# Attention and two feed-forward layers on one core: where a bias is added, when a flag is read, a branch hint, and the place of one sum

## The chip, the cores and the metric

The kernel runs on one core of a Trainium2 chip. The metric is the device time of one execution in microseconds (us), lower is better. The kernel before takes 1094.47 us, the median of three runs.

## What is computed

Local attention with eight global keys and a distance bias, then a feed-forward layer with x·cos(x), then one with a squared ReLU. Cut to what matters:

```python
scores = scale * np.matmul(q, k.transpose(0, 1, 3, 2))          # 4 batches, 8 heads, 768 positions, 64 wide
bias = -slopes[:, None, None] * dist[None, :, :]
scores = np.where(keep, scores + bias, -1e9)                    # keep: first n_global keys, or the last n_local
a = np.exp(scores - np.max(scores, axis=-1, keepdims=True))
x = np.matmul(a / (np.sum(a, -1, keepdims=True) + 1e-9), v)     # -> 3072 tokens of 512
h = x @ w_in;  x = (h * np.cos(h)) @ w_out                      # 512 -> 2048 -> 512
h = np.maximum(x @ w2_in, 0);  out = (h * h) @ w2_out
```

## The kernel before, in words

The 3072 tokens are 24 tiles of 128, and four tiles make a block, six blocks in all. A block goes through attention, through layer one and through layer two. Products in fp32 accuracy are made of fp16 halves: a value is split into a high and a low part, and three products stand for one. Some layers use a scheme with seven block products in the place of eight (P1 to P7), whose outputs are summed on VectorE.

The order of the work is not written out. `fast_path` gives pieces of work to a planner (`plan.add`, `act`, `dve`, `dma`), each with an engine, a cost, a due time and the buffers that it reads and writes. The planner runs through them in a simulated time and then writes the instructions, engine by engine, in the order in which it started the pieces. A table of numbers (`SHIFTS`) moves due times; the change leaves it alone. Because one piece more or less moves every later start in that simulated time, an edit of one piece can reorder others.

**Attention of a tile.** `group` (L891) takes four heads. Six or three matmuls a head give the scores in two PSUM banks of the pool `h`. The bias is added in one of two ways, by `by_pe` (L927):

- By TensorE, for the first three blocks (tiles T below 12). `add_bias` (L865) first puts the bias into the banks, a matmul of the identity with a table of 512 columns for each bank. Then come the scores (L937), `largest` takes the row maximum on VectorE (L878, L882), and ScalarE takes the exponential out of PSUM into the tile `e` (L886).
- By VectorE, for the others. The scores (L922) stand alone, and `reduce` (L942) adds the bias, keeps the row extreme in `nm` and writes the sum into `e` (L946); ScalarE then takes the exponential in place (L954).

There are two tiles of the kind `e`. The first block (T below 4) has its own path, `group32`, and is not touched. Spare matmuls (L1754) fill gaps of TensorE up to 240 us of the planned time.

**The flag.** The kernel is valid for certain ranges of the two inputs `n_global` and `n_local` and of the hidden values; a general path stands behind it in the program for the rest. `farthest` (L1581) finds a bound of the hidden values, `in_range` (L1775) tests everything on VectorE in small instructions, writes an integer `flag_i` (L1791) and at once lets all five engines load it into a register (`values_load`, L1792). At the end of the program `tc.If(ok[0] < 1)` (L1996) branches on that register; in the runs here it skips the general path.

**The end.** In the last stage, products by `second2` (L1348) accumulate in PSUM in the order P1, P2, P6, P5, P7, P4, P3, two of them to a bank, and `gather` (L1383) sums them into the tiles `ta` and `tb`, the two halves of the output rows, by way of `tm` (each sum is an instruction of L1394). `leave2` sends a tile out (L1400).

Of the kernel before, what the change touches and what calls it, by code (L numbers as in the profile page):

```python
# [421 lines left out]


@with_exitstack
def fast_path(ctx, tc, kq, vt, w, n_raw, out, meanwhile):
    nc = tc.nc


# [462 lines left out]
    def group(T, g, x32):  # L891
# [32 lines left out]
                                rhs=kk(z, rows[r], c, c0, n), start=(m == 0), stop=(m == 2),  # L924
                            )

        by_pe = T < 3 * BT  # L927

        def scores_and_bias():

# [452 lines left out]
    def gather(b, n, name, due):  # L1383
        unit = 1.0 / (S_G2 * S_W)
        if name == "P1":
            tiles[b, n] = tuple(new("t" if (b, n) == (TWO[-1], 1) else "v") for _ in range(3))
        ta, tb, tm = tiles[b, n]
        banks = bank_of[b, n]
        flat = lambda t: at(t).rearrange("p a h d -> p (a h d)").bitcast(FP32) if t.pool == "v" else at(t)
        half = lambda t, k: flat(t)[:, 256 * k:256 * k + 256]  # L1390

        def plus(name, dst, dk, src, sk):
            bank = banks[BANK[name][0]]
            dve(due, 0.42, lambda: nc.vector.scalar_tensor_tensor(  # L1394
                out=half(dst, dk), in0=half(bank, BANK[name][1]), scalar=unit, in1=half(src, sk), op0=ALU.mult, op1=ALU.add),
                port=False, r=[bank] if src is dst else [bank, src], w=[dst])

        def leave2(t, d):
            r0 = (b * BT + (2 * d + n if b in SEVEN else 2 * n + d)) * 128
            dma(due + 1, 256, lambda: nc.sync.dma_start(out=out[r0:r0 + 128, :], in_=flat(t)[:, 0:512]), r=[t])  # L1400

        if name == "P1":
            act(due, 256, lambda: nc.scalar.activation(  # L1403
                out=half(tm, 0), in_=half(banks[0], 0), func=ACTF.Copy, scale=unit), r=[banks[0]], new=[tm, ta, tb])
        elif name == "P2":
            plus("P2", ta, 0, tm, 0)
        elif name == "P6":
            plus("P6", tm, 1, tm, 0)
        elif name == "P7":
            plus("P7", tm, 0, tm, 1)  # L1410
            plus("P5", tm, 1, tm, 1)
            plus("P5", tb, 1, tm, 0)
        elif name == "P4":
            plus("P4", tb, 0, tm, 0)
            leave2(tb, 1)
        elif name == "P3":
            plus("P3", ta, 1, tm, 1)
            leave2(ta, 0)

    ROOT = 2.0 ** -11  # L1420
# [160 lines left out]
    def farthest(due):  # L1581
# [18 lines left out]
            nc.vector.tensor_tensor(out=reach[:, 2:3], in0=reach[:, 0:1], in1=reach[:, 1:2], op=ALU.mult)  # L1600

        o = dve(due + 2, 0.6, bound, port=False, r=[ps])
        plan.add((("DVE", 2.0, False),), due + 60, lambda: meanwhile(reach[:, 2:3]), after=[o])

    LAG = 3
    y_all = []
# [168 lines left out]
def in_range(tc, pool, raw, reach):  # L1775

    nc = tc.nc
    f = pool.tile([1, 2, 2], FP32, name="flag_f")
    nc.vector.tensor_copy(out=f, in_=raw[0:1])
    t = pool.tile([1, 7], FP32, name="flag_t")  # L1780
    tests = (
        (f[:, 0, 1:2], 0.0, ALU.is_equal), (f[:, 1, 1:2], 0.0, ALU.is_equal),
        (f[:, 0, 0:1], 0.0, ALU.is_ge), (f[:, 0, 0:1], float(GLOB), ALU.is_le),
        (f[:, 1, 0:1], 1.0, ALU.is_ge), (f[:, 1, 0:1], float(LOC + 1), ALU.is_le), (reach, H_MOST ** 2, ALU.is_le),
    )
    for i, (a, x, op) in enumerate(tests):
        nc.vector.tensor_scalar(out=t[:, i:i + 1], in0=a, scalar1=x, scalar2=None, op0=op)
    r = pool.tile([1, 1], FP32, name="flag_r")
    nc.vector.tensor_reduce(out=r, in_=t, axis=mybir.AxisListType.X, op=ALU.min)
    i = pool.tile([1, 1], INT32, name="flag_i")  # L1790
    nc.vector.tensor_copy(out=i, in_=r)  # L1791
    return nc.values_load(i, min_val=0, max_val=1)  # L1792


@with_exitstack
# [207 lines left out]
```

## Time and profile before

| what | value |
|---|---|
| time, median of 3 runs (lowest, highest) | 1094.47 us (1092.9 to 1095.8) |
| time of the profiled execution | 1094.64 us |
| span of its instructions | 1092.9 us |
| TensorE busy | 1064.8 us, 97% |
| VectorE busy | 802.4 us, 73% |
| ScalarE busy | 750.9 us, 69% |
| GpSimd busy | 247.8 us, 23% |
| DMA, mean | 199 GB/s |

The span runs from the first to the last instruction in the profile; the profiled execution's own time is 1.7 us longer. Busy time of TensorE is taken from the start of a matmul to its modelled end, and neighbours overlap: 512 columns show as 380 ns and follow each other closer than that. What an instruction really takes of the engine is therefore read from start to start.

### The profile page before, as it was taken

The numbers are of one execution on the slowest core, as the hardware profiler recorded it, in microseconds if no ns is written. First come the engines' busy times: TensorE is split into PE (matmuls) and PEld (weight loads), VectorE is DVE, ScalarE is ACT, GpSimd is POOL, SyncE is SP. The second block draws the span as 40 slices with busy tenths as digits, with TensorE's granted clock in tenths as the row PEclk, the third lists the DMA queues.
The fourth block names the chain that finished last, engine by engine and source line by source line (L and its number), as shares of the span: only waits on it lengthen the run. The fifth ranks groups of instructions, "written<-read, shape, count | busy, mean of one in ns | idle before, by whom it ended". The sixth has DMA issues, their size and how long they took to land.

```text
span 1092.9 us, 23235 instructions
## 1 busy us (share of the span) xinstructions
PE 1064.8 (97%) x9396; PEld 755.3 (69%) x9396; DVE 802.4 (73%) x1442; ACT 750.9 (69%) x1349; POOL 247.8 (23%) x193
## 2 busy tenths in 40 slices
PE   6999999999999999999999999999999999999996
PEld 5754545454454444666666689888888888888886
DVE  7999997668687794677886687778368577488372
ACT  6999868887987674765786896455377357366360
POOL 1023320021250210233251221123014224032010
PEclk9999999999999999999999999999999999999998
DMA  6498888647668793778789798787563343334201
GB/s 234 170 239 257 241 284 243 133 88 249 204 185 241 286 349 124 247 226 223 242 263 266 230 236 209 281 289 271 193 221 135 118 147 123 131 123 135 88 2 42
DMA packets 160693, 217.74 MB, mean 199 GB/s; under 512 B 110464, under 2 KB 110976, under 8 KB 159040
## 3 DMA queue, kind: packets, MB, share of 16 engines
q1 hardware_dynamic: 160576, 216.17, 64.2%
q8 instruction: 75, 1.23, 0.5%
q14 instruction: 42, 0.34, 0.1%
HBM read 153.23 MB, written 36.70 MB: 174 GB/s over the span
## 4 chain that ended last, share of the span: by engine, by line
PE 85%; DVE 9%; ACT 4%; issue 1%; DMA 0%; SPq 0%; DVEq 0%; ACTq 0%
PE hps L1232 25%; PE ypps L1141 13%; PE hps L1125 13%; PE ypps L1368 11%; PE ypps L1183 7%; PE ypps L1438 7%; PE hps L983 2%; PE hps L1368 2%; PE hps L922 2%; PE hps L788 1%; DVE dec L65 1%; DVE nm L878 1%; PE hps L937 1%; PE hps L871 1%; DVE dec L68 1%
## 5 line engine op out<-in xcount | busy, mean ns | idle before, releaser
L1232 PEld LDWEIGHTS <-ld 128*128 128x128 f16 x2400 | 234.5, 98 | 35.7 <-issue 2.6
L1232 PE MATMUL hps<-ys,ld 128*128 128x256 f16 x1680 | 196.1, 273 | 1.8 <-DVE t L1426 1.8
L1141 PE MATMUL ypps<-g,ld 128*128 128x512 f16 x768 | 175.8, 379 | 1.6 <-DVE g L474 1.6
L1125 PE MATMUL hps<-xy,w 128*128 128x512 f16 x768 | 174.3, 379 | 1.2 <-DVE x L1000 1.2
L1426 DVE TENSOR_TENSOR t<-hps,t 128x512 f32<-128x512 f32 x160 | 110.0, 688 | 68.8 <-PE hps L1232 65.8
L1141 PEld LDWEIGHTS <-ld 128*128 128x128 f16 x768 | 74.0, 98 | 88.7 <-POOL g L474 1.9
L1125 PEld LDWEIGHTS <-w 128*128 128x128 f16 x768 | 73.7, 98 | 87.7 <-DVE x L1000 1.7
L474 DVE TENSOR_TENSOR g<-t,g 128x512 f16<-128x512 f32 (+1 forms) x129 | 99.6, 777 | 29.9 <-ACT g L1209 29.4
L1209 ACT ACTIVATE g<-t 128x512 f16<-128x512 f32 x128 | 79.3, 623 | 25.1 <-DVE t L1165 23.5
L1183 PE MATMUL ypps<-g,ld 128*128 128x256 f16 x768 | 89.2, 273 | 2.3 <-DVE flag_i L1791 1.8
L1438 PE MATMUL ypps<-ld,g 128*128 128x512 f16 x384 | 90.1, 381 | 0.0
L1183 PEld LDWEIGHTS <-ld 128*128 128x128 f16 x768 | 75.0, 98 | 11.5 <-issue 2.7
L1423 ACT ACTIVATE t<-t 128x512 f32<-128x512 f32 x72 | 45.0, 624 | 48.3 <-DVE t L1426 48.0
L1165 DVE SCALAR_TENSOR_TENSOR t<-t,hps 128x512 f32<-128x512 f32 x72 | 48.9, 681 | 34.1 <-ACT t L1163 34.0
L1161 ACT ACTIVATE t<-hps 128x512 f32<-128x512 f32 x72 | 42.6, 592 | 30.2 <-PE hps L1125 20.8
L1438 PEld LDWEIGHTS <-g 128*128 128x128 f16 x384 | 36.9, 98 | 37.7 <-issue 0.8
L1258 ACT ACTIVATE t<-t 128x512 f32<-128x512 f32 x96 | 60.3, 628 | 2.5
L1163 ACT ACTIVATE t<-t 128x512 f32<-128x512 f32 x96 | 60.3, 628 | 2.3
L474 POOL TENSOR_TENSOR g<-t,g 128x512 f16<-128x512 f32 (+1 forms) x23 | 28.8, 1251 | 142.2 <-ACT g L1209 134.8
L631 POOL TENSOR_TENSOR t<-t 128x256 f32<-128x256 f32 x18 | 16.4, 910 | 158.1 <-DVE x L631 158.0
L1394 DVE SCALAR_TENSOR_TENSOR v<-ypps,v 128x256 f32<-128x256 f32 x49 | 18.6, 419 | 45.2 <-ACT v L1403 37.1
L65 DVE SCALAR_TENSOR_TENSOR dec<-raw,dec 128x1024 int32<-128x1024 int32 x32 | 47.4, 1481 | 0.6
(229 smaller groups left out, 1981.9 us busy)
## 6 DMA issues: line engine op xcount, KB each, us to landing
ld<-w SPq DMA_DIRECT2D x154, 512.0 KB, 4.4
raw<-w SPq DMA_DIRECT2D x32, 1024.0 KB, 6.2
w<-ld SPq DMA_DIRECT2D x44, 512.0 KB, 3.9
ld<-kq SPq DMA_DIRECT2D x23, 512.0 KB, 5.9
ld<-vt SPq DMA_DIRECT2D x24, 256.0 KB, 4.6
yd<-xy SPq DMA_DIRECT2D x6, 1024.0 KB, 5.3
xy<-yd SPq DMA_DIRECT2D x6, 1024.0 KB, 5.9
ld<-w SPq DMA_DIRECT2D x24, 256.0 KB, 3.6
```

The lines of the kernel that those rows point to most:

```text
L65: lambda: nc.vector.scalar_tensor_tensor(out=t, in0=r[:, :, 0], scalar=29, in1=t, op0=ALU.logical_shift_right, op1=ALU.bitwise_or),
L474: op.emit = lambda: eng[op.eng].tensor_tensor(out=out_f(), in0=src_f(), in1=hi_f(), op=ALU.subtract)
L1125: nc.tensor.matmul(out=at(ps), lhsT=w_view(wt)[:, a, j % 2, k * 128:(k + 1) * 128], rhs=x_view(src)[:, c, k, :], start=(n == 0), stop=(n = ...
L1141: nc.tensor.matmul(out=at(y_ps[d]), lhsT=wv[:, a, d * 128:(d + 1) * 128], rhs=at(g)[:, c], start=(j == 0 and n == 0), stop=(j == NJ - 1 an ...
L1163: act(due + 1.2, 512, lambda: nc.scalar.activation(out=at(t), in_=at(t), func=ACTF.Square, scale=HALF_TURN), w=[t])
L1183: nc.tensor.matmul(out=at(y_ps[d])[:, 256 * n:256 * n + 256], lhsT=w_view(wt)[:, a, u, d * 128:(d + 1) * 128], rhs=at(g)[:, z, 256 * u:256 ...
L1209: act(due, 512, lambda: nc.scalar.activation(out=at(g)[:, 0], in_=at(t), func=ACTF.Copy), r=[t], new=[g])
L1232: nc.tensor.matmul(out=at(bank)[:, 256 * u:256 * u + 256], lhsT=wv(a, u, kk), rhs=sv(c, kk), start=(fresh and u == n == 0), stop=(last and ...
L1258: act(due, 512, lambda: nc.scalar.activation(out=at(t), in_=at(t), func=ACTF.Square), w=[t])
L1368: nc.tensor.matmul(out=at(bank)[:, 256 * half:256 * half + 256], lhsT=gv(home)[:, z, c0:c0 + 128], rhs=wv(a, u), start=(q == half == u == ...
L1426: dve(due, 0.7, lambda: nc.vector.tensor_tensor(out=at(t), in0=at(bank), in1=at(u), op=ALU.add), port=False, **k)
L1438: nc.tensor.matmul(out=at(y_ps[d]), lhsT=at(g)[:, z, 256 * u + d % 2 * 128:256 * u + d % 2 * 128 + 128], rhs=wv[:, a, u], start=(q == i == ...
```

## The change

Four edits. The limit of `by_pe` goes from three blocks to two, so that the eight groups of the third block (tiles 8 to 11) take the bias on VectorE. `in_range` returns the flag's tile, and the load into the registers is a piece of work of its own, with a due time 70 us behind that of the test and a `lag` of 40. A branch hint for all five engines is marked ahead of the kernel's work and tied to the branch at the end, which also asks for the general path to be laid next to it. In `gather`, the sum of P5 for the tile `ta` is made when P6 is there and goes into `ta` itself, where it stood behind P7's and went into `tm`. The number of sums stays seven.

```diff
-def fast_path(ctx, tc, kq, vt, w, n_raw, out, meanwhile):
+def fast_path(ctx, tc, kq, vt, w, n_raw, out, judge, ask):
...
-        by_pe = T < 3 * BT
+        by_pe = T < 2 * BT
...
         elif name == "P6":
             plus("P6", tm, 1, tm, 0)
+            plus("P5", ta, 1, tm, 1)
         elif name == "P7":
             plus("P7", tm, 0, tm, 1)
-            plus("P5", tm, 1, tm, 1)
             plus("P5", tb, 1, tm, 0)
         elif name == "P4":
             plus("P4", tb, 0, tm, 0)
             leave2(tb, 1)
         elif name == "P3":
-            plus("P3", ta, 1, tm, 1)
+            plus("P3", ta, 1, ta, 1)
             leave2(ta, 0)
...
         o = dve(due + 2, 0.6, bound, port=False, r=[ps])
-        plan.add((("DVE", 2.0, False),), due + 60, lambda: meanwhile(reach[:, 2:3]), after=[o])
+        o = plan.add((("DVE", 1.0, False),), due + 60, lambda: judge(reach[:, 2:3]), after=[o], lag=40.0)
+        plan.add((("DVE", 0.1, False),), due + 130, ask, after=[o])
...
-    return nc.values_load(i, min_val=0, max_val=1)
+    return i
...
-            ok = []
-            fast_path(tc, *args, n_raw, out, lambda reach: ok.append(in_range(tc, pool, n_raw, reach)))
-            with tc.If(ok[0] < 1):
+            flag, ok = [], []
+            engines = [getattr(mybir.EngineType, e) for e in ("SP", "PE", "DVE", "Activation", "Pool")]
+            tc.mark_branch_hint_location("general", hint=0, engines=engines)
+            fast_path(
+                tc, *args, n_raw, out, lambda reach: flag.append(in_range(tc, pool, n_raw, reach)),
+                lambda: ok.append(nc.values_load(flag[0], min_val=0, max_val=1)))
+            with tc.If(ok[0] < 1, preferred_fallthrough_block=True, label="general"):
                 general_path(tc, *args, n_raw, x_d, out)
```

In the order of the instructions the change shows at three places. The first is VectorE at the first two groups of the third block; before, with `nm` the row maxima and `hps` the banks with scores:

```order
L474 TENSOR_TENSOR g_125<-t_120,g_125 128x512
L878 TENSOR_REDUCE nm_86<-hps_134 128x2
L878 TENSOR_REDUCE nm_86<-hps_135 128x2
L882 TENSOR_SCALAR nm_86<-nm_86 128x4
L878 TENSOR_REDUCE nm_87<-hps_133 128x2
L878 TENSOR_REDUCE nm_87<-hps_136 128x2
L882 TENSOR_SCALAR nm_87<-nm_87 128x4
L474 TENSOR_TENSOR p_96<-e_95,p_96 128x1024
```

And with the change, the first of the two groups and the start of the second:

```order
L474 TENSOR_TENSOR g_132<-t_123,g_132 128x512
L946 ISA e_100,nm_91<-hps_139,bias 128x256
L946 ISA nm_91 128x1
L946 ISA e_100,nm_91<-hps_139,bias 128x256
L946 ISA nm_91 128x1
L946 ISA e_100,nm_91<-hps_140,bias 128x256
L946 ISA nm_91 128x1
L946 ISA e_100,nm_91<-hps_140,bias 128x256
L946 ISA nm_91 128x1
L946 ISA e_99,nm_92<-hps_138,bias 128x256
```

Three instructions of a group became eight, which also write `e`; on TensorE the 16 bias matmuls with their weight loads are gone, and steps of `first` and `second` (L1125, L1141) around the groups of the third and fourth block change places. From the fifth block's attention on, TensorE's order is the same again but for the flag.

The second place is TensorE where it loads the flag; before, between the last matmul of a seven-scheme product (L1232) and the first of a step of `second_quarter` (L1183):

```order
L1232 LDWEIGHTS w_5_111
L1232 MATMUL hps_136<-xy_101,w_5_111 128x256
L1183 LDWEIGHTS ld_68
L1792 TENSOR_LOAD flag_i
L1183 MATMUL ypps_138<-g_128,ld_68 128x256
```

And with the change:

```order
L1183 LDWEIGHTS ld_73
L1183 MATMUL ypps_144<-g_133,ld_73 128x256
L1232 LDWEIGHTS w_2_113
L2000 TENSOR_LOAD flag_i
L1232 MATMUL hps_138<-dec_109,w_2_113 128x256
```

The load moved behind that step, by 24 matmuls and their weight loads; on VectorE, which writes the flag, it moved behind one sum of L1426, and on SP behind one transfer.

The third place is the end of VectorE's work; before, the sums of the last output tiles (`t_121` and `t_120` are `ta` and `tb`, `t_116` is `tm`), with buffer numbers kept:

```order
L1394 SCALAR_TENSOR_TENSOR t_7_121<-hps_2_135,t_2_116 128x256
L1394 SCALAR_TENSOR_TENSOR t_2_116<-hps_0_133,t_2_116 128x256
L1394 SCALAR_TENSOR_TENSOR t_2_116<-hps_1_134,t_2_116 128x256
L1394 SCALAR_TENSOR_TENSOR t_2_116<-hps_0_133,t_2_116 128x256
L1394 SCALAR_TENSOR_TENSOR t_6_120<-hps_0_133,t_2_116 128x256
L1394 SCALAR_TENSOR_TENSOR t_6_120<-hps_1_134,t_2_116 128x256
L1394 SCALAR_TENSOR_TENSOR t_7_121<-hps_3_136,t_2_116 128x256
L1996 COMPARE_AND_BRANCH
```

And with the change (`t_126`, `t_124` and `t_123`):

```order
L1394 SCALAR_TENSOR_TENSOR t_7_126<-hps_0_138,t_4_123 128x256
L1394 SCALAR_TENSOR_TENSOR t_4_123<-hps_1_139,t_4_123 128x256
L1394 SCALAR_TENSOR_TENSOR t_7_126<-hps_1_139,t_4_123 128x256
L1394 SCALAR_TENSOR_TENSOR t_4_123<-hps_2_140,t_4_123 128x256
L1394 SCALAR_TENSOR_TENSOR t_5_124<-hps_1_139,t_4_123 128x256
L1394 SCALAR_TENSOR_TENSOR t_5_124<-hps_2_140,t_4_123 128x256
L1394 SCALAR_TENSOR_TENSOR t_7_126<-hps_3_141,t_7_126 128x256
L2001 COMPARE_AND_BRANCH
```

P5's sum for `ta`, the fourth of seven before, is now the third, ahead of P7's.

## Rows read from the trace of the kernel before

**Rows 1.** The page's first part: busy time, share of span, instructions.

```profile
span 1092.9 us, 23235 instructions
PE 1064.8 (97%) x9396; PEld 755.3 (69%) x9396; DVE 802.4 (73%) x1442; ACT 750.9 (69%) x1349; POOL 247.8 (23%) x193
```

**Rows 2.** The waits of TensorE: us in total, times, longest.

```profile
PE hps L1232 <- DVE t L1426: 2.3, 3, 1.3
...
PE ypps L1183 <- DVE flag_i L1791: 1.8, 1, 1.8
...
PE hps L1125 <- DVE x L1000: 1.2, 1, 1.2
```

**Rows 3.** Timeline of TensorE, a group with bias matmuls: start, length, what.

```profile
177.58 1.03 PE L1141 MATMUL ypps<-g,ld 128*128 128x512 f16 x4
178.44 0.59 PE L871 MATMUL hps<-bias,ident 128*128 128x512 bf16 x2
...
179.82 0.82 PE L1141 MATMUL ypps<-g,ld 128*128 128x512 f16 x3
```

**Rows 4.** Timeline of TensorE, a group without them.

```profile
316.68 0.81 PE L1141 MATMUL ypps<-g,ld 128*128 128x512 f16 x3
317.43 0.34 PE L922 MATMUL hps<-kq 64*128 64x128 f16 x6
...
318.27 0.82 PE L1125 MATMUL hps<-xy,w 128*128 128x512 f16 x3
```

**Rows 5.** Groups of VectorE from 150 to 240 us: busy, mean ns | idle before.

```profile
L878 DVE TENSOR_REDUCE nm<-hps 128x2 f32<-128x512 f32 x16 | 10.3, 683 | 3.4 <-PE hps L937 3.4
L882 DVE TENSOR_SCALAR nm<-nm 128x4 f32<-128x4 f32 x8 | 7.0, 874 | 0.3
```

**Rows 6.** The same view of the whole span, the two instructions of `reduce`.

```profile
L946 DVE CUSTOM_DVE_ANT_0 e<-hps,bias 128x256 f32<-128x256 f32 x64 | 23.2, 420 | 12.4 <-PE hps L922 11.4 <-POOL g L474 1.0
L946 DVE DVE_READ_ACCUMULATOR2_ANT nm<- 128x1 f32 x128 | 10.4, 81 | 0.0
```

**Rows 7.** Timeline at the flag, all engines.

```profile
736.45 0.14 DVE L1791 CAST flag_i<-flag_r 1x1 int32<-1x1 f32 x1
737.15 2.78 PE L1183 MATMUL ypps<-g,ld 128*128 128x256 f16 x24 [1.84 <-DVE flag_i L1791]
```

**Rows 8.** The line of the flag's load: duration min/median/max ns, first and last start.

```profile
L1792 PEldq TENSOR_LOAD <-flag_i x1: 492/492/492, 736.6 to 736.6; - x1
```

**Rows 9.** Timeline of the end: last matmuls, last sums, last transfers.

```profile
1079.67 4.75 PE L1368 MATMUL hps<-w,e 128*128 128x256 f16 x42
...
1083.80 1.87 DVE L1394 SCALAR_TENSOR_TENSOR t<-hps,t 128x256 f32<-128x256 f32 x5 [0.89 <-PE hps L1368]
1085.40 1.12 SPq L1400 DMA_DIRECT2D out<-t  x2
```

**Rows 10.** The branch's line from 1081 us on, columns as in rows 8.

```profile
L1996 SPq EVENT_SEMAPHORE  x8: 17/17/17, 1089.5 to 1090.1; - x8
...
L1996 PEldq COMPARE_BRANCH  x1: 3644/3644/3644, 1082.3 to 1082.3; - x1
...
L1996 DVEq COMPARE_BRANCH  x1: 72/72/72, 1084.8 to 1084.8; - x1
...
L1996 SPq COMPARE_BRANCH  x1: 53/53/53, 1086.6 to 1086.6; - x1
L1996 DVEq EVENT_SEMAPHORE  x1: 21/21/21, 1087.7 to 1087.7; - x1
```

**Rows 11.** The program's closing line, then the last transfers' line from 1085.5 us.

```profile
L1990 SPq EVENT_SEMAPHORE  x10: 17/28/28, 1091.6 to 1092.9; - x10
...
DMA to landing us min/median/max: 2.4/3.1/3.8
```

**Rows 12.** Stretches after 518 us: length, busy by engine, granted clock, DMA share, GB/s.

```profile
518.75:520.06 1.31, 0.00 (x0) 0.02 (x1) 1.31 (x4) 1.31 (x4) 0.00 (x0) 1.00 1.03 432
520.24:523.65 3.41, 3.41 (x15) 1.94 (x14) 3.30 (x20) 3.38 (x7) 0.00 (x0) 0.50 0.50 204
```

## The prediction

> **What bounds the kernel now.** I read the page's busy shares first, then the waits of TensorE, then the timeline at the four places of the change. TensorE is busy for 1064.8 of 1092.9 us, VectorE for 73% and ScalarE for 69% [rows 1]. The waits of TensorE are few and short [rows 2]: after the start of the kernel the largest is 1.8 us for the flag. So, nearly everywhere, time comes off the span when it comes off TensorE, and an engine beside it can take on work as long as it stays ahead. The other place where time can be had is the tail: the last matmul ends at 1079.67 + 4.75 = 1084.4 us [rows 9], and the span ends 8.5 us later.
>
> **Part 1, the bias of the third block.** On TensorE a group with bias matmuls takes 179.82 − 178.44 = 1.38 us up to the next foreign matmul [rows 3], a group without them 318.27 − 317.43 = 0.84 us [rows 4]. The first starts 0.17 us before the end of its forerunner's row (177.58 + 1.03 = 178.61), the second only 0.06 us before it (317.49); so 0.11 us of the 0.54 are lost in starting, and 0.43 are left. Eight groups give 8 × 0.43 = 3.4 us. That is the upper end. The lower end is nothing: all of it comes back as waits for another engine.
>
> What VectorE gets in exchange is about what it loses: 16 reductions and eight scalings, busy for 10.3 and 7.0 us, are (10.3 + 7.0) / 8 = 2.2 us a group [rows 5], against four times 420 and 81 ns, 2.0 us [rows 6]. The scores' banks come free when VectorE is through instead of after the exponential on ScalarE, and TensorE's 1.2 us of waiting for a bank to be emptied (`x` L1000) lies in this stretch [rows 2]. So I take 3.4 us. The planner also reorders neighbours up to the fifth block; that can open or close waits such as this one, and I put it at nothing, with 1.2 us down and 3 us up for the range.
>
> **Part 2, the flag.** Before, TensorE stands still for 1.84 us: VectorE writes the flag by 736.45 + 0.14 = 736.6 us, the load takes 0.49 us, and the matmuls go on at 737.15 [rows 7, 8]. Both new pieces belong to VectorE alone, where the planner applies no `lag`, and the order shows the result: the load is only one step later. On TensorE that step is the 24 matmuls which stood waiting. They would start at 737.15 − 1.84 = 735.3 and run 24 times 109 ns, to 737.9 us. (The 109 ns are the row's length: 2.78 us less the overlap of the last, which I put at 0.16 us, an estimate from that row.) The flag and the load are done at 737.1 us if TensorE's sequencer gets to the load before the engine does. It runs ahead: at the end its branch begins at 1082.3 us, 2.1 us before the last matmul's end [rows 9, 10]. So the load falls under the 24 matmuls, and I take the whole 1.8 us; 1.3 us (1.84 less the 0.49 of the load) if the sequencer is not ahead there, and nothing if the next product is not ready 1.8 us earlier. Next in line is a product of L1232, whose waits for VectorE's sums are 2.3 us in all, in three places [rows 2].
>
> **Part 3, the sum.** The seven sums stay seven, but of the five that follow each other from 1083.80 us [rows 9] one moves ahead, into VectorE's 0.89 us of waiting for P4. Five take 1.87 us, so one step is (1.87 − 0.42) / 4 = 0.36 us, with 420 ns for a single one from like instructions [rows 6]. Both transfers start 0.4 us earlier. It can be nothing only if the transfers' issue binds; SP's pair takes 1.12 us from 1085.40 and the second follows the last sum, so it does not.
>
> **Part 4, the hint.** After its branch at 1086.6 us SP does its next instruction at 1089.5 us; on VectorE the same gap is 1084.8 to 1087.7 us [rows 10]. That is 2.9 us each for a jump. SP is the last engine to branch, and after its eight instructions it pauses again, 1090.1 to 1091.6, before the closing ones that run to 1092.9 us [rows 10, 11]. If the target is there at once, SP waits for the last transfer instead. The two transfers land 2.4 and 3.8 us from issue, middle 3.1 [rows 11]. With the middle, and 0.4 us from part 3: 1085.8 − 0.4 + 3.1 = 1088.5 us, then 0.6 for the eight instructions and 1.3 for the closing ones, 1090.4 us. Without the hint the end is 1092.9 − 0.4 = 1092.5, so the hint is worth 2.1 us. With 3.8 us it is 1.4, with 2.4 us 2.8; nothing if the hint fails. I take the middle, since in the old tail the code for three engines is fetched beside these transfers and I expect less of that. The second pause starts 2.1 us after the first instruction behind the jump would have asked for more (1089.5 to 1091.6) and so hides under the landing.
>
> Five hint instructions are added at the start, one on each engine. The nearest rows are the branches, 53 and 72 ns [rows 10]; I charge 0.1 us, with 0 and 0.2 as ends. The layout request changes nothing: the general path already stands next.
>
> [...]
>
> **The sum.** 3.4 + 1.8 + 0.4 + 2.1 − 0.1 = 7.6 us. The profiled execution took 1094.64 us, so 1087.0 us; the median of the runs is 0.2 us lower, which I leave alone.
>
> **The rivals.**
>
> *The hint does not act.* It is executed once, at the very start, some hundreds of instructions ahead of the branch on SP and 18,000 on TensorE; whatever remembers it must last for the whole kernel. Nothing in the trace of before speaks for or against. Time: 1087.0 + 2.1 = 1089.1 us.
>
> *TensorE's freed time comes back as waits.* The third block gives back time only if VectorE, ScalarE and the transfers can keep up, and at 518.75 us TensorE already waits 1.31 us while VectorE and ScalarE are busy throughout [rows 12]; whoever comes there earlier waits longer. Against it: after the third block TensorE hardly waits for 280 us. Time with part 1 at nothing: 1087.0 + 3.4 = 1090.4 us.
>
> *Slower.* `reduce` now writes `e` on VectorE, where before ScalarE did so later. There are two such tiles; if the one before last is still being split, VectorE stands still, with all that is queued behind it, among them the sums that empty TensorE's banks. [...] Against it: in the later blocks the same instruction was kept waiting by TensorE's scores (11.4 us) and once by GpSimd (1.0 us), never by a tile `e` that had to come free [rows 6].
>
> *The flag gives nothing.* The load is only 2.6 us later, and a product behind it may be as late as the load was: 1087.0 + 1.8 = 1088.8 us.
>
> *The stall at 518 us goes,* as the arrival of TensorE there shifts by some us: 1087.0 − 3.0 = 1084.0 us. The order at that place is unchanged, which speaks against it.
>
> **How the numbers follow.** Forecast 0.52 (between 1085.4 and 1088.6 us), hint without effect 0.18, freed time lost 0.13, stall gone 0.08, flag worth nothing 0.05, slower 0.04. The range goes from 1084.0, with the stall gone, to 1091.2 us, which takes in the hint's failure with up to 2 us of new waits and the loss of part 1. A measurement of this kernel can tell about 0.3% from no change, 3.3 us, so faster means below 1091.2 us. All but the slower case lie there singly; two losses together (1087.0 + 2.1 + 3.4 = 1092.5) do not, and I give such pairs 0.10. Faster 0.86, same 0.10, slower 0.04.
>
> **What would show it.** Part 1: no row of L871 after 120 us, the 64 instances of the 256-wide instruction of L946 [rows 6] become 96 (64 + 8 × 4), and TensorE's busy time falls without new waits between 150 and 440 us. Part 2: no wait of TensorE for `flag_i`, and the load's row without a gap behind it. Part 3: four sums in the last run of L1394, not five. Part 4: SP's first instruction behind its branch follows within some 0.3 us or begins with a long wait for the last transfer. I am wrong if the tail after the last matmul is still over 7.5 us, or if TensorE's idle time grows by more than 2 us anywhere before it.

## The result and the profile after

The changed kernel takes 1084.17 us, the median of four runs (1083.74 to 1085.72); the kernel before, beside it, 1093.68 us. The ratio is 0.9908, with a 95% interval of 0.9896 to 0.9921: 0.9% faster, 8.6 to 11.4 us. Forecast were 1087.0 us, 7.6 us less, with a range down to 1084.0 us. The direction held, and of the four edits two did what was forecast by the way that was forecast (the sum and the hint); the third block gave more than its matmuls, and the flag gave less than half of its forecast. The gain is larger than forecast, and the time stands at the low edge of the range. The profiled execution takes 1085.72 us, 8.9 us less than the profiled one of before.

The page's first part of the kernel after, beside [rows 1]:

```profile
span 1084.0 us, 23236 instructions
PE 1060.6 (98%) x9380; PEld 753.3 (69%) x9380; DVE 802.8 (74%) x1483; ACT 752.9 (69%) x1349; POOL 245.1 (23%) x192
```

TensorE lost 16 matmuls and 4.2 us of busy time; VectorE got 41 instructions and stays at 803 us. Its waits, beside [rows 2]:

```profile
PE hps L1232 <- DVE t L1426: 2.3, 3, 1.3
PE ypps L1141 <- DVE g L474: 1.6, 1, 1.6
PE hps L1232 <- DVE flag_i L1792: 1.1, 1, 1.1
```

The wait of L1125 for `x` L1000 is gone, and the wait for the flag is still there: 1.1 us, where 1.8 stood. A group of the third block, beside [rows 3, 4]:

```profile
188.06 0.34 PE L922 MATMUL hps<-kq 64*128 64x128 f16 x6
...
188.90 2.76 PE L1141 MATMUL ypps<-g,ld 128*128 128x512 f16 x12
```

That is 188.90 − 188.06 = 0.84 us, as in the later blocks. VectorE's groups from 150 to 240 us, beside [rows 5]:

```profile
L946 DVE CUSTOM_DVE_ANT_0 e<-hps,bias 128x256 f32<-128x256 f32 x32 | 11.6, 421 | 4.0 <-PE hps L922 3.9
L946 DVE DVE_READ_ACCUMULATOR2_ANT nm<- 128x1 f32 x32 | 2.6, 83 | 0.0
```

Together 14.2 us, where the maxima and scalings took 10.3 + 7.0 = 17.3 us: VectorE has less to do than before, not the same. The flag, GpSimd's and VectorE's rows and TensorE's wait (start, length):

```profile
728.97 1.16 POOL L474 TENSOR_TENSOR g<-t,g 128x512 f16<-128x512 f32 x1 [7.02 <-ACT g L1209]
729.19 0.95 DVE L1599 TENSOR_SCALAR reach<-reach 1x2 f32<-1x2 f32 x1
...
730.09 2.12 POOL L1281 TENSOR_TENSOR e<-ld 128x1024 f32<-128x1024 f16 x1
730.18 2.03 DVE L1600 TENSOR_TENSOR reach<-reach 1x1 f32<-1x1 f32 x1
...
733.05 0.14 DVE L1792 CAST flag_i<-flag_r 1x1 int32<-1x1 f32 x1
...
733.74 1.47 PE L1232 MATMUL hps<-dec,w 128*128 128x256 f16 x12 [1.10 <-DVE flag_i L1792]
```

VectorE's product of two single numbers (L1600) lasts 2.03 us and ends with GpSimd's L1281. In the kernel before it lasted 0.15 us, and L1281 came behind the flag:

```profile
735.47 0.15 DVE L1600 TENSOR_TENSOR reach<-reach 1x1 f32<-1x1 f32 x1
```

```profile
737.25 2.13 POOL L1281 TENSOR_TENSOR e<-ld 128x1024 f32<-128x1024 f16 x1 [1.83 <-DVE flag_i L1791]
```

The end, beside [rows 9, 10], with the line of the last two transfers below it:

```profile
1073.64 4.75 PE L1368 MATMUL hps<-w,e 128*128 128x256 f16 x42
...
1077.77 1.54 DVE L1394 SCALAR_TENSOR_TENSOR t<-hps,t 128x256 f32<-128x256 f32 x4 [0.43 <-PE hps L1368]
```

```profile
L2001 SPq EVENT_SEMAPHORE  x8: 17/17/17, 1080.5 to 1082.6; - x8
...
L2001 PEldq COMPARE_BRANCH  x1: 418/418/418, 1076.3 to 1076.3; - x1
...
L2001 SPq COMPARE_BRANCH  x1: 73/73/73, 1079.9 to 1079.9; - x1
```

```profile
DMA to landing us min/median/max: 2.5/2.7/2.8
```

Four sums end 1079.31 − 1078.39 = 0.92 us behind the last matmul (1.25 before). SP goes on 0.5 us behind its branch, not 2.9, and its eight instructions are spread over 2.1 us, as they now wait for the last transfer: three of them start before it lands, five behind it. TensorE's own branch takes 0.42 us where it took 3.64. From the last matmul to the end it is 5.6 us instead of 8.5.

One thing has to be known to read these times: the profiles of before and after each hold one stretch of 3.41 us at a granted clock of 0.50. Each stands behind a wait of TensorE (1.31 and 1.60 us), and each costs some 1.7 us, an estimate (half of 3.41). In the profile of before it is at 520 us [rows 12]. That of after has none there, but one at 140 us, where before had 1.00:

```profile
140.05:143.46 3.41, 3.41 (x9) 1.19 (x9) 3.22 (x7) 3.38 (x6) 3.40 (x2) 0.50 0.74 298
514.90:516.40 1.50, 0.23 (x9) 0.15 (x4) 1.50 (x4) 1.50 (x5) 0.00 (x0) 1.00 0.92 386
516.60:520.00 3.40, 3.40 (x23) 2.10 (x22) 3.20 (x20) 3.37 (x7) 0.00 (x0) 1.00 0.37 149
```

The two cancel in the comparison of the profiles. Matmul by matmul (the same matmul's start in both profiles, below called the gain of TensorE's stream), TensorE is 0.2 us earlier at 60 us, 1.5 us later behind the stretch at 140 us, 3.6 us earlier from 242 to 519 us, 5.3 us behind the old profile's stretch, 6.0 us behind the flag and to the end; 2.9 us come from the tail. The third block alone is 3.6 + 1.5 = 5.1 us, the flag 0.7.

### The profile page after: what moved, and what is told of

Its sections match the earlier page's. It is cut to its first block, busy times and chain, and to the rows that moved or that the text cites. A ratio compares the mean times of both kernels' runs of the same rounds, so it can differ in the third digit from the quotient of the medians.

```text
span 1084.0 us, 23236 instructions
## 1 busy us (share of the span) xinstructions
PE 1060.6 (98%) x9380; PEld 753.3 (69%) x9380; DVE 802.8 (74%) x1483; ACT 752.9 (69%) x1349; POOL 245.1 (23%) x192
## 4 chain that ended last, share of the span: by engine, by line
PE 83%; DVE 11%; ACT 4%; issue 1%; DMA 0%; DVEq 0%; SPq 0%; ACTq 0%
PE hps L1232 25%; PE ypps L1141 14%; PE hps L1125 13%; PE ypps L1368 11%; PE ypps L1438 7%; PE ypps L1183 7%; PE hps L922 2%; PE hps L983 2%; PE hps L1368 2%; DVE dec L65 1%; DVE nm L878 1%; DVE dec L68 1%; DVE dec L62 1%; DVE t L1426 1%; DVE xy L474 1%
## 5 line engine op out<-in xcount | busy, mean ns | idle before, releaser
L1232 PEld LDWEIGHTS <-ld 128*128 128x128 f16 x2400 | 234.0, 98 | 35.3 <-issue 2.6
L1232 PE MATMUL hps<-ys,ld 128*128 128x256 f16 x1680 | 195.1, 273 | 1.8 <-DVE t L1426 1.8
L1141 PE MATMUL ypps<-g,ld 128*128 128x512 f16 x768 | 177.8, 382 | 1.6 <-DVE g L474 1.6
L1125 PE MATMUL hps<-xy,w 128*128 128x512 f16 x768 | 174.5, 379 | 0.0
L1426 DVE TENSOR_TENSOR t<-hps,t 128x512 f32<-128x512 f32 x160 | 110.0, 688 | 66.4 <-PE hps L1232 64.3
L1141 PEld LDWEIGHTS <-ld 128*128 128x128 f16 x768 | 74.3, 98 | 90.2 <-issue 2.7
L1125 PEld LDWEIGHTS <-w 128*128 128x128 f16 x768 | 73.9, 98 | 86.2
L474 DVE TENSOR_TENSOR g<-t,g 128x512 f16<-128x512 f32 (+1 forms) x128 | 101.0, 793 | 26.0 <-ACT g L1209 25.2
L1183 PE MATMUL ypps<-g,ld 128*128 128x256 f16 x768 | 89.2, 273 | 0.5 <-DVE g L474 0.5
L1183 PEld LDWEIGHTS <-ld 128*128 128x128 f16 x768 | 75.0, 98 | 9.4 <-issue 0.6
L474 POOL TENSOR_TENSOR g<-t,g 128x512 f16<-128x512 f32 (+1 forms) x24 | 30.8, 1284 | 195.0 <-ACT g L1209 185.1
L954 ACT ACTIVATE e<-e,nm 128x256 f32<-128x256 f32 (+1 forms) x128 | 52.7, 482 | 8.3 <-DVE nm L946 8.1
L946 DVE CUSTOM_DVE_ANT_0 e<-hps,bias 128x256 f32<-128x256 f32 (+2 forms) x128 | 43.2, 395 | 18.0 <-PE hps L922 17.9
```

The lines of the kernel that those rows point to most:

```text
L474: op.emit = lambda: eng[op.eng].tensor_tensor(out=out_f(), in0=src_f(), in1=hi_f(), op=ALU.subtract)
L954: nc.scalar.activation(out=at(e)[:, x, 0:W], in_=at(e)[:, x, 0:W], func=ACTF.Exp, bias=at(nm)[:, x:x + 1], scale=-1.0,)
L1125: nc.tensor.matmul(out=at(ps), lhsT=w_view(wt)[:, a, j % 2, k * 128:(k + 1) * 128], rhs=x_view(src)[:, c, k, :], start=(n == 0), stop=(n = ...
L1141: nc.tensor.matmul(out=at(y_ps[d]), lhsT=wv[:, a, d * 128:(d + 1) * 128], rhs=at(g)[:, c], start=(j == 0 and n == 0), stop=(j == NJ - 1 an ...
L1183: nc.tensor.matmul(out=at(y_ps[d])[:, 256 * n:256 * n + 256], lhsT=w_view(wt)[:, a, u, d * 128:(d + 1) * 128], rhs=at(g)[:, z, 256 * u:256 ...
L1232: nc.tensor.matmul(out=at(bank)[:, 256 * u:256 * u + 256], lhsT=wv(a, u, kk), rhs=sv(c, kk), start=(fresh and u == n == 0), stop=(last and ...
```

## The experiments

Each ratio is against the kernel before, timed with it. "Lowest" is the fastest single run, the one least touched by these stretches; "tail" is from the last matmul to the end of the span.

| kernel | median us | ratio (95%) | lowest us | tail us |
|---|---|---|---|---|
| before, beside the first four | 1094.24 | | 1092.53 | 8.5 |
| after | 1084.17 | 0.9908 (0.9896 to 0.9921) | 1083.74 | 5.6 |
| bias alone | 1088.06 | 0.9945 (0.9932 to 0.9959) | 1087.11 | 8.2 |
| flag alone | 1092.78 | 0.9995 (0.9985 to 1.0005) | 1092.13 | 8.7 |
| hint alone | 1092.12 | 0.9983 (0.9973 to 0.9993) | 1089.87 | 5.8 |
| sum alone | 1092.55 | 0.9984 (0.9975 to 0.9993) | 1092.31 | 8.1 |
| after, bound by reductions | 1083.30 | 0.9897 (0.9882 to 0.9912) | 1082.62 | 5.4 |
| after, hint marked late | 1085.60 | 0.9918 (0.9900 to 0.9935) | 1085.10 | 5.4 |
| after, hint for SP alone | 1085.46 | 0.9921 (0.9903 to 0.9939) | 1084.92 | 6.6 |
| after, second block too | 1089.98 | 0.9960 (0.9945 to 0.9975) | 1089.55 | 5.4 |
| after without the hint | 1087.60 | 0.9931 (0.9914 to 0.9948) | 1086.35 | 7.8 |
| bound by reductions, waits filled | 1082.71 | 0.9887 (0.9871 to 0.9904) | 1082.64 | 5.4 |
| before, scaling by a reduction | 1090.17 | 0.9954 (0.9937 to 0.9970) | 1089.71 | 8.5 |
| all of these together | 1081.42 | 0.9870 (0.9853 to 0.9886) | 1081.10 | 5.7 |

By the lowest runs the four edits alone bring 5.4, 0.4, 2.7 and 0.2 us, 8.7 together; all at once bring 1092.84 − 1083.74 = 9.1 us against the runs of before that stood beside them. Within what a lowest run of 4 to 29 can tell, they add up. Lowest runs compare only within one group of runs: before, the lowest lay between 1092.5 and 1094.6 us from group to group.

**The bias alone.**

```diff
-        by_pe = T < 3 * BT
+        by_pe = T < 2 * BT
```

> The kernel before with the bias edit alone (eight groups take the bias on VectorE). Theory: TensorE's stream in the third block gets 3.4 to 3.6 us shorter (eight groups by 0.43 us), and the 1.3 us of waiting for a bank emptied by L1000 at 192 us goes too, as in the profile with all four edits; nothing comes back behind it. From the first matmul of block three to the fifth block the stream gains 4.8 to 5.0 us, counted without any stretch at the lower clock level; the time is 4.5 to 5 us shorter, ratio about 0.9955. Rival: the freed time comes back as waits between 240 us and the flag at 735 us: then the stream at the flag is less than 2 us earlier than before and the ratio is 0.998 or more. Rival: only the 0.43 us a group are the edit's own and the stall at 192 us was moved by one of the other edits: 3.5 us, ratio 0.997, with the wait for L1000 still there.

TensorE is 0.4 us later than before at 150 us and 4.7 us earlier at 242 us, and stays at 4.7 to the end: 5.1 us from the third block, as with all four edits, and none given back. The wait of L1125 for `x` L1000 is not in its list any more. The first theory holds; both rivals fall.

**The flag alone.**

```diff
-        plan.add((("DVE", 2.0, False),), due + 60, lambda: meanwhile(reach[:, 2:3]), after=[o])
+        o = plan.add((("DVE", 1.0, False),), due + 60, lambda: judge(reach[:, 2:3]), after=[o], lag=40.0)
+        plan.add((("DVE", 0.1, False),), due + 130, ask, after=[o])
```

> The kernel before with the flag edit alone. Theory: on GpSimd the piece L1281 (2.12 us) now stands ahead of the flag's load, where it stood behind it, and it runs while VectorE does the 1x1 product of L1600; that product then takes 2.0 us instead of 0.15, the flag is written 1.9 us later, and TensorE still waits about 1.1 us for it. Gain 0.7 to 0.8 us of TensorE's stream, ratio 0.9993, no difference that the times can show. Rival: the long L1600 came from the third block's reordering, by an accident of timing; then it takes 0.15 us here, TensorE doesn't wait for the flag, and the gain is 1.8 us, ratio 0.9984.

```profile
734.05 2.12 POOL L1281 TENSOR_TENSOR e<-ld 128x1024 f32<-128x1024 f16 x1
```

```profile
734.15 2.03 DVE L1600 TENSOR_TENSOR reach<-reach 1x1 f32<-1x1 f32 x1
...
737.02 0.14 DVE L1792 CAST flag_i<-flag_r 1x1 int32<-1x1 f32 x1
```

The long product is here, without the third block's edit; TensorE waits 1.1 us for the flag and its stream gains 0.7 us: the theory holds. The order on GpSimd shows the cause. Before:

```
L474 TENSOR_TENSOR g_126<-t_119,g_126 128x512
L1792 TENSOR_LOAD flag_i
L1281 TENSOR_TENSOR e_94<-ld_66 128x1024
```

With the flag edit L1281 stands ahead of the load, and so beside VectorE's test.

**The hint alone.**

```diff
+            engines = [getattr(mybir.EngineType, e) for e in ("SP", "PE", "DVE", "Activation", "Pool")]
+            tc.mark_branch_hint_location("general", hint=0, engines=engines)
...
-            with tc.If(ok[0] < 1):
+            with tc.If(ok[0] < 1, preferred_fallthrough_block=True, label="general"):
```

> The kernel before with the hint and the label on the branch alone. Theory: SP's first instruction behind its branch follows within 0.6 us instead of 2.9, the second pause of 1.4 us is gone too, SP then waits for the last transfer, and the tail behind the last matmul shrinks from 8.5 us to 5.9 (the 5.6 of the kernel with all edits and 0.3 for the sum, which isn't here); everything ahead of the tail stays as it was. Ratio 0.9976. Rival: the short tail came from transfers that land earlier, not from the hint: the tail stays over 8 us and the ratio is 1.000.

```profile
L1998 SPq EVENT_SEMAPHORE  x8: 17/17/17, 1087.2 to 1089.2; - x8
...
L1998 SPq COMPARE_BRANCH  x1: 73/73/73, 1086.7 to 1086.7; - x1
```

0.5 us behind the branch, and a tail of 5.76 us: the theory holds. The first matmul starts at 7.17 us, against 7.07 to 7.08 us in the other three runs of one edit, so its price at the start is some 0.1 us; but the profile of before, without a hint, starts at 7.38 us, so this is near what one profile can tell.

**The sum alone.**

```diff
             plus("P6", tm, 1, tm, 0)
+            plus("P5", ta, 1, tm, 1)
...
-            plus("P5", tm, 1, tm, 1)
...
-            plus("P3", ta, 1, tm, 1)
+            plus("P3", ta, 1, ta, 1)
```

> The kernel before with the place of P5's sum alone. Theory: the last sum ends 0.9 us behind the last matmul instead of 1.25, both last transfers leave 0.3 us earlier, but SP fetches its code behind the branch for 2.9 us and pauses again; as that begins 0.3 us earlier too, the span shrinks by 0.3 us: ratio 0.9997, no difference in the times, to be read from the profile's tail alone. Rival: the code fetch, not the transfers, sets the tail and begins at another time: the tail stays 8.5 us within 0.1.

The last sum ends 0.93 us behind the last matmul, as in every profile with the edit; without it, it is 1.25 to 1.26 us. SP's branch, too, comes 1.8 us behind the last matmul, against 2.1 to 2.2 us in the four profiles with neither this edit nor the hint. So far the theory holds: 0.3 to 0.4 us. The tail of 8.1 us doesn't show it by itself, since those four read 8.2 to 8.7 us: from SP's branch to the end it is 6.0 to 6.6 us in all the profiles without the hint. The ratio promises more, 1.7 us, but that isn't the edit's: 11 of these 12 runs lie between 1092.3 and 1092.9 us, the profile has no stretch at the lower clock, and by the lowest runs the gain is 0.2 us. Why this kernel met fewer such stretches stays open.

**The bound by reductions.** The flag's test is freed from what GpSimd does.

```diff
-            nc.vector.tensor_scalar(out=reach[:, 0:2], in0=reach[:, 0:2], scalar1=S_H ** -1, scalar2=None, op0=ALU.mult)
-            nc.vector.tensor_tensor(out=reach[:, 2:3], in0=reach[:, 0:1], in1=reach[:, 1:2], op=ALU.mult)
+            nc.vector.tensor_reduce(out=reach[:, 2:3], in_=reach[:, 0:2], axis=mybir.AxisListType.X, op=ALU.mult)
...
-        (f[:, 1, 0:1], 1.0, ALU.is_ge), (f[:, 1, 0:1], float(LOC + 1), ALU.is_le), (reach, H_MOST ** 2, ALU.is_le),
+        (f[:, 1, 0:1], 1.0, ALU.is_ge), (f[:, 1, 0:1], float(LOC + 1), ALU.is_le), (reach, (H_MOST * S_H) ** 2, ALU.is_le),
```

> The changed kernel with the bound of the hidden values made by two reductions (the second with multiplication; the scale goes into the limit that the bound is tested against) in place of a reduction, a scaling and a 1x1 product; the computation is the same. Theory: the scaling (0.95 us for two numbers) and the product (2.03 us for one) are long because GpSimd's L474 and L1281 run beside them; a reduction is not kept waiting, the flag is written 2.4 to 2.7 us earlier, and TensorE's 1.1 us of waiting for the flag is gone. TensorE's stream behind the flag is 1.1 us earlier, ratio to the kernel before about 0.991 less 0.001, that is 0.990. Rival: what kept VectorE was not GpSimd but the small instructions themselves or the semaphores between them: the new reduction is as long as the product was, and the wait stays at 1 us.

VectorE, and then GpSimd beside it:

```profile
727.46 0.14 DVE L1599 TENSOR_REDUCE reach<-reach 1x1 f32<-1x2 f32 x1
727.53 0.88 DVE L1779 CAST flag_f<-n_raw 1x4 f32<-1x4 int32 x1
...
729.17 0.14 DVE L1791 CAST flag_i<-flag_r 1x1 int32<-1x1 f32 x1
```

```profile
727.25 1.15 POOL L474 TENSOR_TENSOR g<-t,g 128x512 f16<-128x512 f32 x1 [7.02 <-ACT g L1209]
728.36 2.12 POOL L1281 TENSOR_TENSOR e<-ld 128x1024 f32<-128x1024 f16 x1
```

The reduction takes 0.14 us in the middle of GpSimd's L474; the cast behind it is now the one held, until 728.41, just as L474 ends (728.40). TensorE's wait for the flag is gone: against the changed kernel its stream is 1.7 us earlier from 145 us on, where only that one has a stretch at the lower clock, and 3.0 us behind the flag, so 1.3 us are gained there. What was missing of part 2 was GpSimd's. Beside GpSimd's L474 or L1281 VectorE's scaling took 0.95 us, its cast 0.88 us and its product 2.03 us, each to the end of that row within 0.03 us, and the reduction 0.14 us. Not every cast or test beside GpSimd is held: the flag's last cast (0.14 us at 729.17) and the tests ahead of it, on one number each, ran beside L1281 (728.36 to 730.48 us) and took what they took in the kernel before, 0.13 to 0.14 us.

**The hint marked late.** The line that marks it goes from ahead of the kernel's work to just ahead of the branch.

> The changed kernel with the hint marked behind the kernel's work, right ahead of the branch, label and layout kept. Theory: the hint works by letting the code be fetched while the work goes on; marked right ahead of the branch it comes too late on SP, whose gap behind the branch is 2 us or more again, and the tail is about 8.2 us as in the kernel with the sum alone: time 2.5 us above the changed kernel, ratio to the kernel before 0.993. Rival: the layout that the label asks for, not the moment of the hint, made the branch cheap: then the gap stays at 0.5 us and the tail at 5.6.

Nothing was told apart: the hint still stands at 0.8 to 0.9 us on every engine, the stream of TensorE is that of the changed kernel within 0.2 us, and the tail 5.4 us. Where it is marked in the source does not set where it stands, and whether the code comes while the work goes on was not shown.

**The hint for SP alone.**

```diff
-            engines = [getattr(mybir.EngineType, e) for e in ("SP", "PE", "DVE", "Activation", "Pool")]
+            engines = [getattr(mybir.EngineType, e) for e in ("SP",)]
```

> The changed kernel with the hint for SP alone. Theory: SP is the last to branch and alone sets the end; the other four fetch their code within 4 us of branches that they reach 1.5 us and more before SP's end, so the tail stays at 5.6 us within 0.3 and the time is that of the changed kernel. Rival: the closing barrier waits for the engine whose code arrives last, and with VectorE's branch at 1078.4 us and 2.9 us of fetching it comes to the barrier at 1081.5 us, still ahead of SP's last wait at 1082.3; only if the fetches take over 4 us does the tail grow, by up to 1 us.

```profile
L2001 SPq EVENT_SEMAPHORE  x8: 17/17/17, 1079.1 to 1081.8; - x8
...
L2001 PEldq COMPARE_BRANCH  x1: 3464/3464/3464, 1074.5 to 1074.5; - x1
L2001 DVEq COMPARE_BRANCH  x1: 72/72/72, 1076.7 to 1076.7; - x1
...
L2001 DVEq EVENT_SEMAPHORE  x1: 21/21/21, 1079.7 to 1079.7; - x1
```

```profile
DMA to landing us min/median/max: 2.4/3.1/3.8
```

The theory missed: the tail is 6.6 us. SP goes on at once, but the last transfer lands 3.8 us from issue, where it was 2.8 us with all five hinted. The rival's 1 us is right, its reason isn't: VectorE's first instruction behind its branch ran at 1079.7 us, 1.8 us ahead of the last landing. What is late is the transfer. From 1072 us on the DMA's two instruction queues moved 7 packets here, 4 in the changed kernel and 9 in that of before. That such packets delay the transfer is argued from the runs with and without hints (for the slower transfer, 2.6 to 2.9 us with the hint on all engines, 3.7 to 4.8 us in the others) and not shown by itself.

**The second block, too.**

```diff
-        by_pe = T < 2 * BT
+        by_pe = T < BT
```

> The changed kernel with the limit of by_pe at one block, so that the second block's eight groups, too, take the bias on VectorE. Theory: between 60 and 140 us VectorE is busy for 90 to 99% of the time, but in the third block its busy time did not grow with this edit (160 to 240 us: 50.7 us against 54.2 before), as the maxima and scalings that go cost as much as the reductions that come; so TensorE's stream gets 3 to 4 us shorter once more and the ratio to the kernel before is about 0.988. Rival: with VectorE so near its limit, steps that write e as they reduce come late, and TensorE's waits for VectorE between 50 and 160 us (3.5 us in the changed kernel) grow by more than the 3.4 us that are saved: ratio 0.991 or more.

```profile
PE ypps L1141 <- DVE g L474: 5.1, 2, 4.8
PE hps L1125 <- DVE xy L474: 1.3, 1, 1.3
```

The theory missed, and the rival holds by its signs: TensorE's waits for VectorE's splits (L474) in the second block's neighbourhood go from 1.6 to 6.4 us, and its stream ends 4.3 us later than the changed kernel's. The same edit pays in the third block, where VectorE was busy for 64 of 90 us (150 to 240 us), and costs in the second, where it is busy for over 90%. That the full VectorE is the cause is argued, not shown, for two more things differ in this run. The planner puts 56 spare matmuls on TensorE where it put 32 (rows of 13.9 us instead of 7.9). And in VectorE's queue ahead of the longest wait a split took 3.14 us, where the four others of its form took 1.2, with a GpSimd split beside it. What each costs isn't told apart.

**Without the hint, with the label.** The line that marks the hint is left out.

> The changed kernel without the hint instruction; label and requested layout of the branch stay. (In the run called late hint the instruction turned out to stand first on every engine, as in the changed kernel, wherever it is marked in the source; it told nothing.) Theory: the hint instruction alone makes the branch cheap: SP's gap behind its branch is 2.9 us again, the last two transfers land after 3 us or more instead of 2.5 to 2.7, and the tail behind the last matmul is 8.1 us as in the kernel with the sum alone; the first matmul starts 0.1 us earlier, at 7.08 us. Rival: label and layout suffice: the gap stays at 0.5 us and the tail at 5.5.

```profile
L2000 SPq EVENT_SEMAPHORE  x8: 17/17/17, 1082.9 to 1083.8; - x8
...
L2000 SPq COMPARE_BRANCH  x1: 53/53/53, 1080.0 to 1080.0; - x1
```

2.9 us again; the last transfer lands 4.2 us from issue, and the tail is 7.8 us. The hint does it, the label nothing. (The first matmul starts at 7.15 us here, so the hint's price at the start is not over 0.1 us.)

**Two waits filled.** On the kernel with the bound by reductions.

```diff
+                    steps[0] += 1
+                    if steps[0] == 121:
+                        spin(y_ps[d], 7, False)
...
+            steps[1] += 1
+            if steps[1] == 28:
+                spin(opened[-1], 5, False)
...
+            opened.append(y_ps[d])
```

> The kernel of the run on the bound, with spare matmuls (of zeros, 512 columns, added to a sum that is open) in the two waits of TensorE behind which stretches at the lower clock level were seen: seven at 138 us, where it waits 1.6 us, and five at 513 us, where it waits 1.3 us. They are new work that changes no result. Theory: the stretches of 3.41 us at a granted clock of 0.50 that some executions show behind one of these waits (140 us, 520 us) come from the standstill; with the waits filled they are gone there, so the profile shows none between 25 us and the end, the waits themselves cost what they did, and the runs lie closer together: none over 1084.5 us, median 1082.5 to 1083, the lowest as without the matmuls (1082.6) within 0.3. What stays are the stretches in the first 25 us. Rival: these stretches come whether TensorE stands still there or not; then they show in some of these executions too, at the same places, and the spread is as wide as that of the kernel before (4 us) with the median at 1083.3 or above.

```profile
140.04:143.50 3.46, 3.46 (x17) 1.56 (x17) 3.26 (x7) 3.42 (x8) 3.37 (x2) 1.00 0.75 297
...
515.00:519.00 4.00, 4.00 (x27) 2.44 (x26) 3.80 (x21) 3.97 (x8) 0.00 (x0) 1.00 0.32 129
```

All four runs lie between 1082.64 and 1083.10 us; the lowest is, within 0.02 us, that of the kernel without the fill (1082.62), whose five went up to 1084.47 us. The stretch that the profile still shows starts at 15.2 us. Of the twelve profiles of kernels without the fill, seven have a stretch behind one of these two waits; this one and that of the last run below, with the fill, have none. The theory holds so far as a few executions can show it: with TensorE at work in these two waits no stretch was seen behind them.

**The scaling by a reduction.** On the kernel before, to see where the bias edit's 5.1 us come from beyond the 3.4.

```diff
+        nc.vector.memset(pairs, -SCALE)
...
-                out=at(nm)[:, 2 * r:2 * r + 2], in_=at(ps[r]).rearrange("p (i c) -> p i c", i=2)[:, :, 0:W],
+                out=pairs[:, 2 * r:2 * r + 2, 0], in_=at(ps[r]).rearrange("p (i c) -> p i c", i=2)[:, :, 0:W],
...
-        nc.vector.tensor_scalar(out=at(nm), in0=at(nm), scalar1=-SCALE, scalar2=None, op0=ALU.mult)
+        nc.vector.tensor_reduce(out=at(nm), in_=pairs, axis=mybir.AxisListType.X, op=ALU.mult)
```

> The kernel before with the scaling of the row maxima (L882) made by a reduction with multiplication over pairs of a maximum and a constant; the bias stays where it was, the computation is the same. Theory: the 1.25 us that TensorE waits at 192 us for a bank emptied by L1000 come from the scaling at 190.8 us, which took 1.99 us instead of 0.17 because GpSimd's L474 (190.64 to 192.76 us) ran beside it; a reduction is not kept waiting, so every one of the 24 takes under 0.2 us, the wait at 192 us is gone, and TensorE's stream behind it is 1.2 us earlier: ratio 0.999. That is the part of the bias edit's gain that went beyond the matmuls saved. Rival: the wait came from the order of the work there, which only the bias edit changes: the scalings get short, but TensorE waits at 192 us as long as before, or at another place nearby.

In the kernel before, at TensorE's wait of 192 us, GpSimd and VectorE:

```profile
190.64 2.12 POOL L474 TENSOR_TENSOR kq<-ld,kq 128x1024 f16<-128x1024 f32 x1 [9.13 <-ACT kq L696]
```

```profile
190.80 1.99 DVE L882 TENSOR_SCALAR nm<-nm 128x4 f32<-128x4 f32 x1
```

With the reduction, all 24 of them (L884 here):

```profile
L884 DVE TENSOR_REDUCE nm<-pairs x24: 160/161/163, 12.6 to 230.6; 128x4 f32<-128x8 f32 x24
```

The scalings had taken 0.17 to 1.99 us, and every one over 0.18 us had GpSimd's L474 beside it. The wait at 192 us is gone, and the stream gains 1.4 us there and 1.3 us more between 45 and 100 us, where the theory had named nothing. (The ratio, 0.9954, flatters it: its profile has no stretch at the lower clock, and the runs of before beside it start at 1094.6 us.)

**All together**, the scaling added to the kernel with the waits filled.

> The kernel with the bound by reductions and the spare matmuls in two waits, with the scaling of the row maxima made by a reduction over pairs, too; the computation is the same. Here the scaling is left in the first two blocks alone, where some of the 16 took 0.8 to 1.1 us beside GpSimd in the kernel before. Theory: in those blocks TensorE's waits for the tile e behind the scalings (3.2 us in four places) shrink by the 0.6 to 0.9 us by which the scalings get shorter, at one or two places: the stream gains up to 1 us, median 1082 us, ratio 0.988. Rival: those waits end with ScalarE's own queue, and the scaling was not the last to come: no difference, 1082.7 us.

The stream gains 1.2 us, all of it between 45 and 140 us: a little more than the theory's 1 us. At 1081.42 us (ratio 0.9870) this kernel is the fastest of all those here, the changed one included.

## Why the prediction came out as it did

**Part 1 was right in its term and wrong in what it put at nothing.** The third block gave 5.1 us; without the 1.4 us that the run of the scaling puts down to the wait at 192 us, 3.7 us are left for the matmuls saved, against 3.4. The step that failed is the sentence on the reordered neighbours, "I put it at nothing, with 1.2 us down": the wait of 1.2 us did go, and 0.3 us more came that no run explains. The wait hung on a scaling that GpSimd held for 1.8 us. The edit takes the scalings out of the third block, and `reduce` was not held: of its 66 additions of the bias that ran beside GpSimd in the changed kernel none took over 430 ns. The run of the scaling shows that freeing the scaling is enough. But the work was reordered there, too: the GpSimd split that held the scaling is not at this place in the changed kernel, whose GpSimd has no work from 164.7 to 194.1 us. With the scaling left in, the wait might have gone as well; no run tells the two apart. The sign stood in [rows 5]: 874 ns for four numbers a lane, which the prediction multiplied without asking why.

**Part 2 failed.** "I take the whole 1.8 us" became 0.7. The step that failed is the time at which the flag is written: it was taken over from [rows 7], and the load alone was moved. The section on the change names TensorE, VectorE and SP as the queues in which the load moved; it moved on GpSimd too, past L1281, which then ran beside the test and made it 1.9 us longer. The ends that were named, 1.3 us and nothing, were for other reasons (a sequencer that is not ahead, a product that is not ready). The run of the bound gives the rest back.

**Part 3 was right**: the last sum and SP's branch come 0.3 to 0.4 us earlier, against 0.4, and there are four sums at the end.

**Part 4 was right in its mechanism and short by 0.6 us.** SP waits for the last transfer instead of 2.9 us behind its branch, as forecast. The hint is worth 8.5 − 5.8 = 2.7 us, not 2.1 (in profiles whose tails without it lie between 8.2 and 8.7 us). Two terms of the sum were mis-sized. The landing was taken as 3.1 us, the middle of 2.4 and 3.8; the slower of the two lands 2.6 us from issue with the hint alone and 2.8 us in the changed kernel. From 1072 us on the DMA's two instruction queues moved 9 packets in the profile of before, 5 with the hint alone and 4 in the changed kernel; that the transfer lands earlier for that reason is argued, not shown. And the 0.6 us for SP's eight instructions were put behind the landing as a whole; three of the eight run ahead of it, and the other five take 0.3 us. The price at the start, charged as 0.1 us, is not over that. SP went on 0.5 us behind its branch with the hint and 2.9 us without, on the same label, and the first rival falls.

**The other rivals.** No freed time came back as waits behind the third block. The slower case did not come either: VectorE's `reduce` waited for scores alone, never for an `e`. The standstill at 518 us did not go, it is 1.3 us in both profiles; what went there, in this execution, is the stretch at the lower clock behind it, and one came at 140 us instead. The 3.0 us of this rival are an estimate from [rows 12], 1.31 us idle and half of 3.41 us; that the measured time lies beside its 1084.0 us is chance.

The sum by profiles: 5.1 (third block) + 0.7 (flag) + 2.9 (tail) + 0.2 (start) = 8.9 us, against 3.4 + 1.8 + 2.5 − 0.1 = 7.6. So the misses are +1.7, −1.1, +0.4 and +0.3 us; that they partly cancel is luck, and the last is scatter of the start. The medians differ by 9.5 us, as the profiled execution of after is the longest of its four: the other three (1083.7 to 1084.3 us) lie about one stretch of 1.7 us below it, while that of before lies 1.0 us above its median.

## What to carry to other kernels

When a tiny VectorE instruction takes 0.9 or 2 us, look for a GpSimd row that ends when it does; if there is one, write the instruction as a reduction (0.14 and 0.16 us here). When a step is moved, walk every queue that it is moved past, GpSimd's too, and ask what now runs beside the chain that you count on. A branch at the end is worth a hint on every engine, not only on the last one to branch: here the tail was 5.6 us with all five, 6.6 us with SP's alone and 7.8 us with none.

## What the runs showed of the hardware

SP's first instruction behind its branch came after 2.9 us without a hint and after 0.5 us with one given some 1080 us earlier, and without hints on all engines the slower of the last two transfers took 3.7 to 4.8 us to land instead of 2.6 to 2.9 us. GpSimd's `TENSOR_TENSOR` held a `TENSOR_SCALAR` (0.95 and 1.99 us), a `CAST` (0.88 us) and a `TENSOR_TENSOR` (2.03 us) of VectorE until its own end (to 0.03 us in the cases shown), and not the reductions put in their place (143 ns for the product; 160 to 163 ns in all 24 scalings made that way); the flag's last cast and tests of one number beside it were not held (0.13 to 0.14 us). Behind a standstill of TensorE of 1.31 us (before) and of 1.60 us (after) the granted clock was 0.50 for 3.41 us, some 1.7 us each by the estimate above; with spare matmuls in the two waits the runs spread over 0.5 us instead of 1.9 us (1082.6 to 1084.5).
